# Keys of the last three batches: loaded in rows and turned over by DMA transpositions instead of TensorE

## The chip, the core and the metric

The kernel runs on one core of a Trainium2 chip. A core has five engines that run side by side and meet only at semaphores: TensorE (PE in the profile; its weight loads are shown apart as PEld), VectorE (DVE), ScalarE (ACT), GpSimd (POOL) and SyncE (SP), which here does nothing but issue transfers. Sixteen DMA engines carry the transfers. The metric is the time of one execution on the device, in microseconds (us); lower is better.

## The reference, cut to what matters

Attention over eight batches of eight heads, with 16 "beacon" keys and values put ahead of the 576 others, feeds a gated feed-forward network (called FFN below).

```python
B, H, S, Nb, D = (8, 8, 576, 16, 64)
k_all = concatenate([beacon_k, k], axis=2)          # 592 keys
v_all = concatenate([beacon_v, v], axis=2)
scores = scale * q @ k_all.T                        # causal; beacons are always seen
a = softmax(scores)
attn = a @ v_all
x = attn.transpose(0, 2, 1, 3).reshape(4608, 512)
out = (relu(x @ w_gate) * (x @ w_val)) @ w_out      # d_ff = 1536
```

Queries, keys, values and weights come from DRAM in float32; the kernel rounds them to bfloat16 for TensorE.

## The kernel before, in words

**One batch of attention.** `new_batch` makes the loads of a batch and what prepares them; `tile_step` and `group` do its scores, softmax and product with the values.

- Queries and keys are loaded by `load_pair`, one transfer for a pair of heads: 512 positions, four neighbouring positions of a head joined in one piece of 1 KB (L522). POOL rounds the tile to bfloat16 (`rounded`, L487), TensorE turns it over with four products with the identity (`turned`, L499), and ACT or DVE copies the result out of PSUM (`copy`, L439 for ACT, L441 for DVE) into `kT`, the transposed keys, or into `diag`, the queries of two heads set block-diagonally.
- The positions that `load_pair` leaves over come with `load_rest`: "first" holds 48 query rows and the 16 beacon keys (64 rows), "last" the last 64 keys and 16 queries (80 rows). Both go the same way: cast, four products of 64 or 80 columns, three copies.
- Values are loaded in rows by `load_v` (L596 to L599), in five chunks of up to 128 positions, each position with all eight heads: 128 pieces of 8 times 256 bytes. POOL rounds a chunk (L443), and it is used as it is.
- A step of scores (L657, L660, L665) multiplies queries by transposed keys. The query blocks are named A to D (of 128 positions), E (64) and F (the last 16 positions of all heads). AB sees up to 256 keys, C 384, D 512, E and F nearly all. DVE takes the row minimum (L677, L680), ACT the exponential and its sum (L691), DVE the inverse (L705), POOL scales (L712). A DMA transposition (L758) turns the probabilities `pb` of a pair of heads, 25 blocks of 128 by 128, into `pTb`; TensorE multiplies by the values (L768; L797 for F, from `pTf`), and ACT or DVE copies the result into `xT`.

**The FFN.** `hidden` (L835) multiplies `xT` by the gate and value weights, ACT applies the relu (L839), DVE multiplies (L843); `project` (L855) multiplies by the output weights, ACT or DVE copies to `osb`, and SP stores it (L868).

**What sets the order.** Nothing is run in the order in which it is written. Every piece is a task of `Plan` with the engines it may take, a booked cost, its dependencies, the buffers it holds, and a rank. `Plan.order` walks through booked time: of all tasks that could begin it takes the one that begins first, ties broken by rank. The result is one fixed order of instructions for each engine. An engine never goes past an instruction that waits. FFN tasks have ranks from 1000 up, so TensorE takes them when no attention is ready. `RANK` and `AHEAD` rank the loads and the preparing of a batch (the fourth entry serves batches 3 to 7), `WHOLE` and `F_RANK` its steps, `PACE` gives the earliest booked time of a step, `LAZY` is how long the planner lets a product with the values lie ready while other work can be had.

**Buffers.** Seven tiles `st` receive loads, three tiles `h16` hold rounded rows, there are two `kT`, two `diag`, two `v16`, three `pb`, three `pTb`, one `pf` and one `pTf`, and eight PSUM banks.

**Queues.** All loads, all transpositions and all but three stores are issued by SP, in one order. A transposition that waits for its source holds up everything behind it.

Of the kernel before, what the change touches and what calls it, by code (L numbers as in the profile page):

```python
# [10 lines left out]
BF16 = mybir.dt.bfloat16  # L11
# [6 lines left out]


BACKLOG = 3.0  # L20
EARLIER = {('g', 0): 3, ('v', 0): 4, ('g', 1): 2}
RANK = (-1.46, -25.77, -19.88, -17.37)
AHEAD = (-24.27, 8.0, -0.29, 8.0)
W_ISSUE = 0.8
W_MOVE = 3.1
W_FROM = 14.62
# [12 lines left out]
FILL_BANK = 36.0  # L39
SWITCH = 0.1  # L40
LAGS = {"PE": 0.22, "ACT": 0.16, "DVE": 0.14, "POOL": 0.1, "DMA": 0.1}
LAZY = 22.34
LAZY1 = 32.19
SLOT_LAZY = 0
ON_PE = 1
# [9 lines left out]
ORDER0 = "q0 q1 F k0 k1 k3 v1 q3 k2 q2 v2 v3 L v0 v4"  # L55
ORDER1 = "k0 F q0 k2 L k3 q2 v3 q3 k1 v0 v2 q1 v1 v4"
ORDER = "q0 k1 L k0 F q3 k3 q1 v1 k2 v0 v4 v3 q2 v2"
N_ST = 7
F_RANK = (6.53, 8.48, -1.67, 11.78)
CASTS = ('POOL', 'DVE')  # L60
N_OSB = 4
STEPS = {0: [(['AB'], (-4.55, -4.2, -4.25, -5.72)), (['C'], (-2.2, 4.89, 0.9, 1.36)), (['D', 'E'], (-0.26, 1.73, 10.1, -3.41))],
         1: [(['AB'], (4.7, -5.26, -1.44, -4.08)), (['C'], (8.45, 11.63, 1.33, -5.23)), (['D', 'E'], (3.48, 1.1, 9.61, 4.15))],
         2: [(['AB'], (6.63, 0.38, 0.63, -2.81)), (['C', 'D', 'E'], (6.95, 10.43, 5.74, -0.2))]}
WHOLE = (0.99, 5.23, 4.5, 5.2)
CUTS = {0: (240,), 1: (240,), 2: (240,), 3: ()}
LAST_PARTS = 2
FIRST_MOST = 4
PACE0 = 0.0
HOLD = {0: (0.0, 0.0, 0.0), 1: (0.0, 0.0, 35.39)}  # L70
PACE = 31.01


class Slots:
# [72 lines left out]
class Plan:  # L147
# [7 lines left out]
    def add(self, engines, cost, run, deps=(), holds=(), prio=0.0, lag=None, part=False, lazy=0.0, after=0.0, move=0.0):  # L155
        t = Task(engines if isinstance(engines, tuple) else (engines,), cost, run, deps, holds, prio, lag, part, lazy, move)
        t.ready = after
        for d in t.deps:
            d.users.append(t)
        self.tasks.append(t)  # L160
        return t
# [107 lines left out]
def kernel(  # L269
# [12 lines left out]
    nc = tc.nc  # L282
    B, H, S, D = q.shape
    Nb = beacon_k.shape[2]
# [3 lines left out]
    P = 128  # L288
    NP = H // 2
    SK = Nb + S  # L290
    NC = (SK + P - 1) // P
# [5 lines left out]
    neg_scale = -1.0 / (D ** 0.5)  # L297
# [17 lines left out]
    def many(n, shape, dtype, name):  # L315
        return [cp.tile(shape, dtype, name=f"{name}{i}") for i in range(n)]
# [4 lines left out]
    scales = cp.tile([P, 2], FP32, name="scales")  # L321
# [12 lines left out]
             for i in range(11)]  # L334
    p_t[0], pT_t[0], p_t[2], pT_t[2] = early[:3], early[3:5], early[5:8], early[8:]
    p_s, pT_s = [Slots(t) for t in p_t], [Slots(t) for t in pT_t]
    kT_s = Slots(many(2, [P, NP, SK], BF16, "kT"))
    v_s = Slots(many(2, [P, NC, DM], BF16, "v16"))
    diag_s = Slots(diag_t)
    stage_s = Slots(many(N_ST, [P, DM], FP32, "st"))  # L340
    outs = Slots(many(N_OSB, [P, DM], FP32, "osb"))
    osb_s = outs
    cast_s = Slots(many(3, [P, DM], BF16, "h16"))
# [8 lines left out]

    plan = Plan(BACKLOG)
    add = plan.add


    def c_dve(n):
        return 0.07 + 0.00104 * n
# [7 lines left out]
    def c_act(n):  # L366
        return 0.06 + 0.00083 * n
# [69 lines left out]
    def copy(e, dst, src):  # L437
        if e == "ACT":
            nc.scalar.copy(dst, src)  # L439
        elif e == "DVE":  # L440
            nc.vector.tensor_copy(dst, src)  # L441
        else:
            nc.gpsimd.tensor_scalar(dst, src, 1.0, 1.0, ALU.mult, ALU.mult)  # L443
# [17 lines left out]
    def heads(src, b, s0, sl):  # L461
        return src[b, :, s0:s0 + sl, :].rearrange("h s d -> s h d")
# [6 lines left out]
    def new_batch(b, prio, work):  # L469
        t = Batch()  # L470
        t.b = b
        t.kT = Hold(kT_s, 2 * (NP + 2) + NP * 4 + 1)
        t.v = Hold(v_s, NC + NP * (len(STEPS[b]) if b in STEPS else 2) + 1)
        t.diag = Hold(diag_s, 3 * NP + 6 + NP * 4 + 1)
        t.rows = {}
# [1 line left out]
        def rounded(into, st, rows, by, prio, ld, order):  # L477

            h16 = Hold(cast_s, 2)

            def shrink(x):
                to = order(h16.tile)[:rows]
                of = st.tile[:rows] if rows < P else st.tile.rearrange("p (h j d) -> p h j d", h=2, j=4)
                if x.engine == "ACT":
                    nc.scalar.activation(to, of, AF.Copy, scale=by)
                else:
                    (nc.gpsimd if x.engine == "POOL" else nc.vector).tensor_scalar(to, of, by, 1.0, ALU.mult, ALU.mult)  # L487

            return h16, add(eng, cost, shrink, (ld, on_scales), (st, h16, *into), prio[1])

        def turned(h16, rows, ca, prio, users):
            ps = Hold(first_ps if b == 0 else v_ps, 1 + users)
            deep = P if b else rows

            def turn(_):
                for a in range(4):

                    to = ps.tile[:, a * P:a * P + rows]
                    nc.tensor.matmul(to, h16.tile[:deep, a * P:(a + 1) * P], ident[:deep, :rows],  # L499
                                     start=True, stop=True)  # L500

            return ps, add("PE", c_pe(4 * rows), turn, (ca, on_ident), (h16, ps), prio[1])

        gate = (weight_in[GATE],) if b else ()
# [6 lines left out]
        eng = CASTS if b == 0 else ("POOL",)  # L511
        cost = {"POOL": 0.6, "DVE": 0.45, "ACT": 0.55}
        MAIN = 4 * P
        REST = S - MAIN
# [37 lines left out]
        def load_rest(kind, prio):  # L552

            st = Hold(stage_s, 2)
            own = 64 - Nb if kind == "first" else TAIL
            pieces = {"first": [(q, 0, own), (beacon_k, 0, Nb)], "last": [(k, MAIN, REST), (q, S - TAIL, own)]}[kind]
            rows = sum(x[2] for x in pieces)
            qs, ks = (0, own) if kind == "first" else (REST, 0)

            def fetch(_):  # L560
                s3 = st.tile.rearrange("p (h d) -> p h d", h=H)
                at = 0
                for src, s0, n in pieces:
                    gated(nc.sync.dma_start(s3[at:at + n], heads(src, b, s0, n)))
                    at += n

            ld = add("DMA", (1.05, 0.012 * rows if b else 1.55 if kind == "first" else 1.2, 8 * rows), fetch, gate, (st,), prio[0])
            i = 0 if kind == "first" else 1
            h16, ca = rounded((t.kT, t.diag), st, rows, scales[:rows, i:i + 1], prio, ld, lambda t_: t_)
            ps, tu = turned(h16, rows, ca, prio, 3)  # L570

            def evict_k(x):
                at = 0 if kind == "first" else Nb + MAIN
                n = rows - own
                copy(x.engine, t.kT.tile[:, :, at:at + n], ps.tile.rearrange("p (a n) -> p a n", a=NP)[:, :, ks:ks + n])

            def evict_q(x, hh):
                ps3 = ps.tile.rearrange("p (a n) -> p a n", a=NP)
                r = slice(64 * hh, 64 * hh + 64)
                at = 64 * hh + Nb if kind == "first" else NQ * P + TAIL * hh  # L580
                copy(x.engine, t.diag.tile[r, :, at:at + own], ps3[r, :, qs:qs + own])

            n = NP * (rows - own)
            t.rows["k", kind] = [add(("ACT", "DVE"), {"ACT": c_act(n), "DVE": c_dve(n)}, evict_k, (tu,), (ps, t.kT), prio[1])]
            n = NP * own
            t.rows["q", kind] = [add(("ACT", "DVE"), {"ACT": 0.06 + c_act(n), "DVE": 0.06 + c_dve(n)}, lambda x, hh=hh: evict_q(x, hh),
                                     (tu, on_zeros.get(b)), (ps, t.diag), prio[1]) for hh in range(2)]

        def load_v(c, prio):
            st = Hold(stage_s, 2)  # L590
# [11 lines left out]
            t.rows["v", c] = add(eng, cost, lambda x: copy(x.engine, t.v.tile[:rows, c, :], st.tile[:rows]),  # L602
                                 (ld,), (st, t.v), prio[1])

        for at, what in enumerate((ORDER0, ORDER1, ORDER)[min(b, 2)].split()):
            pr = (prio + 0.01 * at, work + 0.01 * at)
            if what in "FL":
                load_rest({"F": "first", "L": "last"}[what], pr)
            elif what[0] == "v":
                load_v(int(what[1]), pr)  # L610
            else:
                load_pair(what[0], int(what[1]), pr)
# [5 lines left out]
    def tile_step(t, p, name, ph, sc, prio, after, blocks):  # L618

        deps = [x for i in ([*range(NP)] if name == "F" else [p]) + (["first", "last"] if name in "EF" else ["first"])  # L620
                for kind in "kq" for x in t.rows[kind, i]]
        if name == "F":

            deps += [x_done[0, "AB", i] for i in range(NP)]
# [2 lines left out]
        if name in "EF":  # L627
            n = SK - TAIL if name == "E" else SK
# [7 lines left out]
        else:  # L636
            offs = [0, 0]
            for x in name:
                for hh in range(2):
                    n = P * FULL[x] + 64 * (hh + 1)  # L640
# [47 lines left out]
        for i, (n, hh, _, _, _, a) in enumerate(parts):  # L688
# [5 lines left out]
            need = [last[1]] if name in "EF" else [x for x, y in zip(lows, parts) if y[1] == hh]  # L694
# [185 lines left out]
    for b in range(B):  # L880
        batches.append(new_batch(b, RANK[min(b, 3)] + b * T0, AHEAD[min(b, 3)] + b * T0))
    for b in range(B):
        steps = STEPS.get(b, [(["AB", "C", "D", "E"], WHOLE)])
        for i, (names, ranks) in enumerate(steps):
# [9 lines left out]
    for b in range(B):  # L894
        hT = [Hold(hid_s, len(CUTS.get(b, ())) + 1 + REG // P) for _ in range(NF)]
        cuts = [0, *CUTS.get(b, ()), REG]
        prio = 1000 + 10.0 * b
# [8 lines left out]
    for i in range(2):  # L906
        b0, b1 = i * B // 2, (i + 1) * B // 2
        w = (b1 - b0) * (S - REG)
        prio = 1000 + 10.0 * b1 - 5.0
        hT = [Hold(hid_s, 1 + w // P + (LAST_PARTS - 1) * i) for _ in range(NF)]  # L910
        deps = [x for b in range(b0, b1) for x in done(b, REG, S)]
        hid = hidden(lambda ki, b0=b0, b1=b1: ends[:, ki, b0:b1, REG:], w, 0, deps, hT, prio)
        for t0 in range(0, w, P):
            b = b0 + t0 // (S - REG)
# [7 lines left out]
    order = plan.order()  # L922
    for i, (key, n) in enumerate(EARLIER.items()):
        at = order.index(weight_task[key])
# [38 lines left out]
```

## Time and profile before

| | before |
|---|---|
| median of 3 runs | 407.43 us (405.87 to 408.02) |
| the profiled execution, its time | 406.38 us |
| its span, first to last instruction | 404.7 us |
| mean granted TensorE clock | 0.999 |
| DVE, ACT, POOL busy | 78%, 72%, 58% |
| moved by DMA | 68.03 MB, mean 168 GB/s |

Between the time of an execution and its span lie 1.7 us before the first and after the last instruction.

How the views are read. The page gives the busy time of each engine and, in 40 slices, its share in tenths. The list of waits says who waited for whom and how long. The chain of waits follows the end of the kernel back, step by step, to what released it; in order of time its rows are start, length, and what ran ("PE f L835 x4" is four products of line 835 that write a PSUM bank f). Groups of instructions give count, busy time, and the mean of one in ns. "SPq" is SP's queue of transfers: the length of such a row is how long SP was taken by issuing it, and the time from issue to landing is listed apart.

### The profile page before, as it was taken

Reading aid. Unit: us, or ns where it says so; the run is one execution under the profiler, and the core shown is the slowest. Engines: PE = TensorE matmul, PEld = TensorE weight load, DVE = VectorE, ACT = ScalarE, POOL = GpSimd, SP = SyncE. Lnnn points to the kernel's source line nnn. Section 1 sums busy time; section 2 is a strip of 40 time slices with the busy share of each in tenths; the row PEclk is TensorE's granted clock in tenths of the full one; section 3 lists DMA queues with packets and bytes.
Section 4 is the critical chain, followed back from the end, with each engine's and each line's share of the span. In section 5 each row is a group of like instructions: output and inputs, shape, how many; then the busy total and the mean of one; then the engine's idle time right before and its main releaser. Section 6 shows DMA issues by size and latency. Waiting matters only on the chain.

```text
span 404.7 us, 10380 instructions
## 1 busy us (share of the span) xinstructions
PE 392.9 (97%) x3276; PEld 246.9 (61%) x3311; DVE 314.8 (78%) x1160; ACT 289.5 (72%) x958; POOL 233.9 (58%) x434
## 2 busy tenths in 40 slices
PE   7799999999999999999999999999999999999996
PEld 5567877587766877545558744554554545444484
DVE  7898999889989988899998998787988634233252
ACT  5799989789888968797988789998858433033030
POOL 5899885957777667687975966875737300000000
PEclk9999999999999999999999999999999999999999
DMA  7999999999889999999999999999296640110111
GB/s 230 181 232 217 222 173 189 198 240 213 178 183 228 214 181 236 183 228 200 247 204 198 231 212 188 252 200 198 71 164 126 152 90 0 53 52 0 53 52 54
DMA packets 172616, 68.03 MB, mean 168 GB/s; under 512 B 146832, under 2 KB 168080, under 8 KB 172560
## 3 DMA queue, kind: packets, MB, share of 16 engines
q1 hardware_dynamic: 167568, 62.38, 75.1%
q0 software_dynamic: 4752, 4.72, 7.2%
q8 instruction: 26, 0.43, 0.5%
q14 instruction: 30, 0.25, 0.2%
q10 hardware_dynamic: 240, 0.26, 0.2%
HBM read 38.27 MB, written 9.44 MB: 118 GB/s over the span
## 4 chain that ended last, share of the span: by engine, by line
PE 86%; POOL 5%; ACT 3%; issue 2%; DVE 2%; DMA 1%; SPq 0%; POOLq 0%; ACTq 0%; DVEq 0%
PE f L835 43%; PE f L855 22%; PE f L665 7%; PE f L768 5%; PE f L499 4%; ACT xT L691 2%; PE f L657 2%; POOL pb L712 1%; POOL xT L712 1%; PE f L919 1%; PE f L797 1%; DMA st<-in_beacon_k_dram 1%; POOL h L487 1%; PE f L660 1%; PE f L747 1%
## 5 line engine op out<-in xcount | busy, mean ns | idle before, releaser
L712 POOL TENSOR_SCALAR pb<-pb,small 128x576 bf16<-128x576 bf16 (+8 forms) x224 | 122.2, 562 | 54.9 <-DVE small L705 47.5
L691 ACT ACTIVATE pb<-f,small 128x64 bf16<-128x64 f32 (+6 forms) x256 | 131.3, 525 | 18.4 <-DVE small L680 14.3
L680 DVE CUSTOM_DVE_ANT_0 f<-f,mask 128x128 f32<-128x128 f32 (+7 forms) x256 | 111.7, 476 | 8.9 <-PE f L665 5.6
L839 ACT ACTIVATE g<-f 128x512 f32<-128x512 f32 (+3 forms) x156 | 72.1, 471 | 65.0 <-PE f L835 63.9
L835 PE MATMUL f<-xT,wv_r 128*128 128x512 bf16 (+3 forms) x616 | 111.8, 313 | 0.6
L835 PE MATMUL f<-xT,wg_r 128*128 128x512 bf16 (+3 forms) x619 | 109.5, 313 | 0.3
L843 DVE TENSOR_TENSOR hT<-g,f 128x512 bf16<-128x512 f32 (+3 forms) x156 | 80.2, 519 | 37.2 <-PE f L835 33.6
L855 PE MATMUL f<-wo_r,hT 128*128 128x512 bf16 (+1 forms) x423 | 102.0, 373 | 1.0
L835 PEld LDWEIGHTS <-wg_r 128*128 128x128 bf16 x624 | 60.0, 98 | 32.4 <-issue 0.3
L835 PEld LDWEIGHTS <-wv_r 128*128 128x128 bf16 x624 | 59.4, 98 | 32.8 <-issue 0.8
L855 PEld LDWEIGHTS <-hT 128*128 128x128 bf16 x444 | 41.6, 98 | 38.9
L691 ACT ACTIVATION_READ_ACCUMULATOR pb<-f,small 128x1 f32 x256 | 54.0, 211 | 0.0
L665 PE MATMUL f<-kT,diag 128*128 128x384 bf16 (+7 forms) x255 | 47.0, 286 | 1.6 <-DVE diag L441 0.5
L680 DVE DVE_READ_ACCUMULATOR2_ANT small<- 128x1 f32 x296 | 41.4, 140 | 0.0
L487 POOL TENSOR_SCALAR h<-st 128x512 bf16<-128x512 f32 x62 | 38.0, 620 | 3.3 <-DMA st<-in_q_dram 1.4
L441 DVE COPY osb<-f 128x512 f32<-128x512 f32 (+1 forms) x26 | 17.6, 677 | 23.1 <-PE f L855 22.7
L712 POOL TENSOR_SCALAR xT<-xT,small 128x64 bf16<-128x64 bf16 (+4 forms) x64 | 27.5, 448 | 9.1 <-ACT xT L691 4.0
L441 DVE CAST diag<-f 64x512 bf16<-64x512 f32 (+2 forms) x45 | 26.7, 592 | 4.0 <-PE f L499 1.4
L499 PE MATMUL f<-ident,h 128*128 128x128 bf16 (+3 forms) x320 | 27.9, 218 | 1.8 <-ACT pb L691 0.8
L439 ACT CAST diag<-f 64x512 bf16<-64x512 f32 (+2 forms) x51 | 22.7, 445 | 9.4 <-PE f L499 3.8
L665 PEld LDWEIGHTS <-diag 128*128 128x128 bf16 x256 | 20.4, 98 | 14.5 <-issue 1.4
L499 PEld LDWEIGHTS <-h 128*128 128x128 bf16 (+1 forms) x320 | 20.8, 99 | 13.9 <-POOL h L487 6.8
(67 smaller groups left out, 377.8 us busy)
## 6 DMA issues: line engine op xcount, KB each, us to landing
st<-in_q_dram SPq DMA_DIRECT2D x32, 256.0 KB, 4.1
st<-in_k_dram SPq DMA_DIRECT2D x32, 256.0 KB, 4.4
out_dram<-osb SPq DMA_DIRECT2D x32, 256.0 KB, 2.4
st<-in_v_dram SPq DMA_DIRECT2D x24, 256.0 KB, 4.6
st<-in_v_dram SPq DMA_DIRECT2D x8, 224.0 KB, 4.9
wg_r<-in_moe_w_gate_dram POOLq DMA_DIRECT2D x3, 512.0 KB, 6.8
wv_r<-in_moe_w_val_dram POOLq DMA_DIRECT2D x3, 512.0 KB, 10.0
wo_r<-in_moe_w_out_dram POOLq DMA_DIRECT2D x3, 512.0 KB, 10.6
```

The costliest lines, as they stand in the source:

```text
L439: nc.scalar.copy(dst, src)
L441: nc.vector.tensor_copy(dst, src)
L487: (nc.gpsimd if x.engine == "POOL" else nc.vector).tensor_scalar(to, of, by, 1.0, ALU.mult, ALU.mult)
L499: nc.tensor.matmul(to, h16.tile[:deep, a * P:(a + 1) * P], ident[:deep, :rows], start=True, stop=True)
L665: nc.tensor.matmul(view(i), t.diag.tile[:, p, j * P:j * P + P], kT[:, p, :n], start=True, stop=True)
L680: nc.vector.tensor_tensor_reduce(out=view(i), in0=view(i), in1=msk, scale=1.0, scalar=small["t"][:, 0:1] if name in "EF" else 3.0e38, op0= ...
L691: nc.scalar.activation(ph.tile.rearrange("p a n -> p (a n)")[:, a:a + n], view(i), AF.Exp, bias=small["t"][:, low:low + 1], scale=-1.0, ac ...
L712: (nc.gpsimd if x.engine == "POOL" else nc.vector).tensor_scalar(one, one, small["t"][:, 8 + i:9 + i], 1.0, ALU.mult, ALU.mult)
L835: nc.tensor.matmul(to, w_r[:, ki, nf * P:(nf + 1) * P], x, start=(ki == 0), stop=(ki == KM - 1))
L839: r = add("ACT", c_act(w), lambda _, psg=psg, g=g: nc.scalar.activation(g.tile[:, :w], psg.tile[:, :w], AF.Relu), (a,), (psg, g), -1000 + ...
L843: hid.append(add("DVE", c_dve(w), lambda _, psv=psv, g=g, nf=nf: nc.vector.tensor_mul(hT[nf].tile[:, c0:c0 + w], g.tile[:, :w], psv.tile[: ...
L855: nc.tensor.matmul(ps.tile[:, :w], hT[nf].tile[:, t0:t0 + P], wo_r[:, nf, n0:n0 + w], start=(nf == 0), stop=(nf == NF - 1))
```

## The change

For batches 5, 6 and 7 (`FROM = 5`) keys no longer go through `load_pair` and `load_rest`. They are loaded like values, in five chunks of up to 128 positions with all heads (`load_k`), rounded by POOL into an `h16` tile, and turned over by a DMA transposition of that tile, four blocks of 128 by 128, straight into `kT`. The tile `kT` is widened from 592 to 640 columns so that the last chunk fits. "First" and "last" carry queries alone in these batches (48 and 16 rows). A step of scores there depends on the key chunks it sees: AB on chunks 0 and 1, C on 0 to 2, D on 0 to 3, E and F on all five. A new order of loads (`ORDER_N`) serves these batches, and some ranks and planner numbers are changed; all ranks changed here serve batches from 3 on.

```diff
+ORDER_N = "q0 k1 q3 q1 k0 k3 v1 F k2 v3 L q2 v2 v0 v4"
+FROM = 5
+V_MOVE = 1.54
-RANK = (-1.46, -25.77, -19.88, -17.37)
-AHEAD = (-24.27, 8.0, -0.29, 8.0)
+RANK = (-1.46, -25.77, -19.88, 41.4)
+AHEAD = (-24.27, 8.0, -0.29, 57.18)
-LAZY = 22.34
+LAZY = 24.06
-F_RANK = (6.53, 8.48, -1.67, 11.78)
+F_RANK = (6.53, 8.48, -1.67, 23.02)
-WHOLE = (0.99, 5.23, 4.5, 5.2)
+WHOLE = (5.03, 5.84, 11.83, 8.03)
-PACE = 31.01
+PACE = 29.69
...
-    kT_s = Slots(many(2, [P, NP, SK], BF16, "kT"))
+    kT_s = Slots(many(2, [P, NP, NC * P], BF16, "kT"))
...
+            if b >= FROM:
+                pieces = [x for x in pieces if x[0] is q]
...
+        def load_k(c, prio):
+            st = Hold(stage_s, 2)
+            rows = min(P, SK - P * c)
+            def fetch(_):
+                s3 = st.tile.rearrange("p (h d) -> p h d", h=H)
+                if c == 0:
+                    nc.sync.dma_start(s3[:Nb], heads(beacon_k, b, 0, Nb))
+                    nc.sync.dma_start(s3[Nb:], heads(k, b, 0, P - Nb))
+                else:
+                    nc.sync.dma_start(s3[:rows], heads(k, b, P * c - Nb, rows))
+            ld = add("DMA", (1.1 if c == 0 else 0.55, V_MOVE * rows / P, 8 * rows), fetch, gate, (st,), prio[0])
+            h16 = Hold(cast_s, 2)
+            ca = add(eng, cost, lambda x: copy(x.engine, h16.tile[:rows], st.tile[:rows]), (ld,), (st, h16), prio[1])
+            t.rows["K", c] = [add("DMA", (1.22, 0.177 * NP), lambda _: nc.sync.dma_start_transpose(
+                t.kT.tile[:, :, P * c:P * c + P], h16.tile), (ca,), (h16, t.kT), prio[1] - 100.0)]
...
+            if b >= FROM and what[0] == "k":
+                load_k(int(what[1]), pr)
+                if what[1] == "3":
+                    load_k(4, pr)
...
+        if t.b >= FROM:
+            need = {"AB": 2, "C": 3, "D": 4}.get(name, NC)
+            deps += [x for c in range(need) for x in t.rows["K", c]]
```

The built program, counted without its times: TensorE has 48 instruction pairs (weight load and product) fewer, the 48 products of 128 columns that turned over 12 key tiles; 12 products shrink from 64 to 48 columns and 12 from 80 to 16. ACT and DVE lose 18 copies into `kT`. POOL has three casts more (15 key chunks for 12 key pairs). SP issues 15 transpositions more. The orders of all engines are the same as before up to a point about half way (TensorE: the scores of batch 4) and differ from there on.

More of the change, by code (lines that the diff above doesn't have):

```diff
@@ L471, in new_batch @@
         t.b = b
-        t.kT = Hold(kT_s, 2 * (NP + 2) + NP * 4 + 1)
+        t.kT = Hold(kT_s, (NC if b >= FROM else 2 * (NP + 2)) + NP * 4 + 1)
         t.v = Hold(v_s, NC + NP * (len(STEPS[b]) if b in STEPS else 2) + 1)
@@ L556, in load_rest @@
             pieces = {"first": [(q, 0, own), (beacon_k, 0, Nb)], "last": [(k, MAIN, REST), (q, S - TAIL, own)]}[kind]
+            if b >= FROM:
+                pieces = [x for x in pieces if x[0] is q]
             rows = sum(x[2] for x in pieces)
-            qs, ks = (0, own) if kind == "first" else (REST, 0)
+            qs, ks = (0, own) if kind == "first" else (0 if b >= FROM else REST, 0)
             def fetch(_):
@@ L568, in load_rest @@
             i = 0 if kind == "first" else 1
-            h16, ca = rounded((t.kT, t.diag), st, rows, scales[:rows, i:i + 1], prio, ld, lambda t_: t_)
-            ps, tu = turned(h16, rows, ca, prio, 3)
+            h16, ca = rounded((t.diag,) if b >= FROM else (t.kT, t.diag), st, rows, neg_scale if b >= FROM else scales[:rows, i:i + 1],
+                              prio, ld, lambda t_: t_)
+            ps, tu = turned(h16, rows, ca, prio, 2 if b >= FROM else 3)
             def evict_k(x):
@@ L583, in load_rest @@
             n = NP * (rows - own)
-            t.rows["k", kind] = [add(("ACT", "DVE"), {"ACT": c_act(n), "DVE": c_dve(n)}, evict_k, (tu,), (ps, t.kT), prio[1])]
+            if b >= FROM:
+                t.rows["k", kind] = []
+            else:
+                t.rows["k", kind] = [add(("ACT", "DVE"), {"ACT": c_act(n), "DVE": c_dve(n)}, evict_k, (tu,), (ps, t.kT), prio[1])]
             n = NP * own
@@ L587, in load_rest @@
                                      (tu, on_zeros.get(b)), (ps, t.diag), prio[1]) for hh in range(2)]
+        def load_k(c, prio):
[6 more added lines that the diff above has]
+                    nc.sync.dma_start(s3[Nb:], heads(k, b, 0, P - Nb))
+                else:
+                    nc.sync.dma_start(s3[:rows], heads(k, b, P * c - Nb, rows))
[4 more added lines that the diff above has]
+                t.kT.tile[:, :, P * c:P * c + P], h16.tile), (ca,), (h16, t.kT), prio[1] - 100.0)]
         def load_v(c, prio):
@@ L603, in load_v @@
                                  (ld,), (st, t.v), prio[1])
-        for at, what in enumerate((ORDER0, ORDER1, ORDER)[min(b, 2)].split()):
+        for at, what in enumerate((ORDER0, ORDER1, ORDER, ORDER_N)[3 if b >= FROM else min(b, 2)].split()):
             pr = (prio + 0.01 * at, work + 0.01 * at)
-            if what in "FL":
+            if b >= FROM and what[0] == "k":
+                load_k(int(what[1]), pr)
+                if what[1] == "3":
+                    load_k(4, pr)
+            elif what in "FL":
                 load_rest({"F": "first", "L": "last"}[what], pr)
@@ L620, in tile_step @@
         deps = [x for i in ([*range(NP)] if name == "F" else [p]) + (["first", "last"] if name in "EF" else ["first"])
-                for kind in "kq" for x in t.rows[kind, i]]
+                for kind in "kq" for x in t.rows.get((kind, i), [])]
+        if t.b >= FROM:
+            need = {"AB": 2, "C": 3, "D": 4}.get(name, NC)
+            deps += [x for c in range(need) for x in t.rows["K", c]]
         if name == "F":
```

## The prediction

> **What bounds the kernel now.** I read the page first, then the chain, then TensorE's waits, then the stretches that the change touches.
>
> ```profile
> span 404.7 us, 10380 instructions
> PE 392.9 (97%) x3276; PEld 246.9 (61%) x3311; DVE 314.8 (78%) x1160; ACT 289.5 (72%) x958; POOL 233.9 (58%) x434
> ...
> DMA  7999999999889999999999999999296640110111
> ...
> PE 86%; POOL 5%; ACT 3%; issue 2%; DVE 2%; DMA 1%; SPq 0%; POOLq 0%; ACTq 0%; DVEq 0%
> ```
>
> ```profile
> PE f L919 <- POOL mask L384: 1.9, 1, 1.9
> ...
> PE f L665 <- DVE diag L441: 0.5, 1, 0.5
> PE f L665 <- ACT diag L439: 0.5, 1, 0.5
> ```
>
> ```profile
> core 0: us, PE busy (x) PEld busy (x) DVE busy (x) ACT busy (x) POOL busy (x), PEclk, DMA share, GB/s
> ...
> 200.00:232.00 32.00, 31.84 (x326) 22.25 (x327) 29.19 (x115) 26.36 (x95) 24.16 (x44) 1.00 1.07 217
> 232.00:264.00 32.00, 31.84 (x244) 17.14 (x247) 28.17 (x103) 29.02 (x96) 23.01 (x45) 1.00 1.15 213
> 264.00:296.00 32.00, 31.79 (x237) 16.85 (x241) 26.14 (x101) 26.09 (x85) 21.99 (x41) 1.00 0.79 148
> 296.00:322.00 26.00, 25.78 (x183) 13.30 (x186) 19.90 (x77) 18.14 (x61) 12.09 (x22) 1.00 0.72 153
> ```
>
> TensorE carries 86% of the chain, and its longest waits after the start are two of 0.5 us, both on copies of queries. From 200 to 322 us, where batches 5 to 7 are worked on, it is idle for 0.75 of 122 us, at the full granted clock. Here a product taken away is time won, as long as TensorE finds its next input ready. The other resource near its limit is the transfers: their share is above 1 (packets overlap) until 264 us, 0.79 and 0.72 after. A late transfer does not show in the chain now, because FFN work stands ahead of each wait.
>
> **The change part by part.** *Products removed.* The chain in order of time has the price:
>
> ```profile
> 224.24 0.22 PE f L499 x4
> ...
> 229.97 0.48 PE f L499 x12
> ...
> 265.19 0.12 PE f L499 x4
> ```
>
> Four products of 128 columns take 0.22 us, four of 64 take 0.12 (265.19). The row of x12 holds groups of 128, 80 and 64 columns, so 80 columns cost 0.48 - 0.22 - 0.12 = 0.14. Twelve key tiles go: 12 x 0.22 = 2.64 us. Of "last", 80 columns become 16: between 0.14 - 0.12 = 0.02 (if 16 cost as much as 64) and 0.14 x 64/80 = 0.11 each; of "first", 64 become 48: 0 to 0.03 each. Three of both: 0.1 to 0.4. Products removed: 2.7 to 3.0; I take **-2.8 us**.
>
> *Copies removed, casts added.*
>
> ```profile
> L487 POOL TENSOR_SCALAR h<-st 128x512 bf16<-128x512 f32 x62 | 38.0, 620 | 3.3 <-DMA st<-in_q_dram 1.4 <-PE f L835 0.9 <-PE f L499 0.6
> ...
> L441 DVE CAST kT<-f 128x512 bf16<-128x512 f32 x18 | 12.2, 680 | 0.1
> ...
> L439 ACT CAST kT<-f 128x512 bf16<-128x512 f32 x14 | 8.3, 592 | 1.8 <-PE f L499 1.7
> ```
>
> The 12 large copies are 12 x 0.59 to 0.68 = 7 to 8 us of ACT and DVE. They shorten nothing that TensorE waits for beyond the two 0.5 us rows above: 0 to -1 us. I take 0, as both rows name queries, which stay. POOL gains 3 casts, 3 x 0.62 = 1.9 us, covered by its 41 idle us between 200 and 322 (122 less 81 busy): 0. Without that cover it would be 1.9.
>
> *Transfers.* Key bytes are the same, in smaller pieces:
>
> ```profile
> DMA packets 172616, 68.03 MB, mean 168 GB/s; under 512 B 146832, under 2 KB 168080, under 8 KB 172560
> ```
>
> ```profile
> st<-in_k_dram SPq DMA_DIRECT2D x32, 256.0 KB, 4.4
> ...
> st<-in_v_dram SPq DMA_DIRECT2D x24, 256.0 KB, 4.6
> ...
> st<-in_q_dram SPq DMA_DIRECT2D x8, 96.0 KB, 3.8
> pTb<-pb SPq DMA_TRANSPOSE x28, 6.2
> ...
> xT<-xT SPq DMA_TRANSPOSE x12, 3.5
> ...
> pTf<-pf SPq DMA_TRANSPOSE x7, 3.5
> ```
>
> ```profile
> L758 SPq DMA_TRANSPOSE pTb<-pb x28: 1494/3970/6172, 60.9 to 321.6; - x28
> L758 SPq DMA_TRANSPOSE xT<-xT x12: 1210/1261/2384, 54.1 to 116.0; - x12
> L758 SPq DMA_TRANSPOSE pTf<-pf x7: 1201/1271/2720, 76.3 to 304.6; - x7
> ...
> DMA to landing us min/median/max: 2.6/5.6/8.2
> ```
>
> A batch's 592 keys are 592 x 8 = 4,736 pieces of 256 B, where before 4 pair loads were 1,024 pieces of 1 KB and the 80 keys left over 640 of 256 B: 4,736 - 1,664 = 3,072 pieces more a batch, 9,216 in all, 5% of the 172,616 packets. Value chunks have exactly this shape and land after 4.6 us, key pairs after 4.4, so I price a key load 0.2 us later. A four-block key transposition is not in the trace. From below it cannot take SP less than 1.2 us, what the five-block `pTf` takes at least, or land before 2.6; from above 2.7 us on SP and 8.2 to landing, the worst rows. I take 1.27 and 3.5, the medians of five and six blocks. Fifteen of them are 19 us of SP over some 150. The last batch's attention ends some 10 us later in the new order, but with FFN work in between; what counts is whether each input is there when TensorE comes to it.
>
> *The new waits.* I laid the changed order of TensorE end to end at the chain's pace (four products of 512 columns in 0.86 us, others in proportion) and shifted it so that the old order, laid out alike, meets the old trace (18 to 19 us of start and gaps). This places instructions; the inputs' times are summed from rows:
>
> ```profile
> 222.61 0.47 SPq L564 DMA_DIRECT2D st<-in_q_dram  x1
> ...
> 234.57 1.19 SPq L868 DMA_DIRECT2D out_dram<-osb  x2
> ```
>
> ```profile
> 313.93 0.24 PE f L657 x2
> ...
> 341.15 1.50 PE f L768 x32
> ...
> 343.62 10.14 PE f L855 x47
> ```
>
> ```profile
> 319.06 0.75 POOL L712 TENSOR_SCALAR pb<-pb,small 128x576 bf16<-128x576 bf16 x1 [1.82 <-DVE small L705]
> ```
>
> From the last score of a pair (ends 314.17) to POOL's last scaling of it (ends 319.81) are 5.6 us: the link from TensorE to SP's transposition. A load issue is 0.47 us, a store 0.6, a 25-block transposition 3.97.
>
> - Batch 5, "first" queries: the last pair of batch 4 is scored to 195.6; +5.6 = 201.2. SP then issues a `pTb`, a `pTf`, two key transpositions, four stores and a value load ahead of "first": 3.97 + 3 x 1.27 + 2.4 + 0.47 = 10.7, so 211.9; +3.8 landing, +0.62 cast = 216.3. TensorE turns them at 217.9: **1.6 us to spare**.
> - Batch 7, third key chunk: a pair of batch 6 is scored to 281.1; +5.6, +3.97 for its transposition = 290.7; chunk 0 takes two issues, 4.6 and 0.62 to 296.9; then on SP its transposition, one `pTb`, two stores, two key transpositions: 1.27 + 3.97 + 1.2 + 2.54 = 9.0, so 305.9; +3.5 = 309.4. The first C scores stand at 311.6: **2.2 us**.
> - Batch 7, last values: the last pair is scored to 337.2; +5.6 + 6.2 = 349.0; its values stand at 349.8: **0.8 us**. Before, 27 us lie between these two (313.93 to 341.15), and 10 us of `project` for batch 6 stood behind the values (343.62). In the new order those products stand ahead of the last values, and behind them comes batch 7's own FFN: whatever is late here moves the end by as much.
>
> So margins shrink from tens of us to 0.8 to 2.2, each a sum of some eight links. I price waits at 0 if every sum holds, and up to 8.2 - 3.5 - 2.2 = 2.5 at the chunk and 2.0 (8.2 for 6.2) - 0.8 = 1.2 at the end. I take **+1.0** in all: near the lower end, because all three sums come out ahead.
>
> The sum is -2.8 + 1.0 = -1.8 on the profiled execution's 406.38, 404.6. The median of the runs, 407.43, lies 1.05 above that execution, so in its terms **405.6 us**.
>
> **The rivals.**
>
> - *No new wait.* The margins hold, and nothing else changes: -2.8, 404.6 against the median. For it: each sum is positive, and the shares of 0.79 and 0.72 leave room for transfers of batches 6 and 7. Against it: batch 5's keys are fetched at shares above 1.
> - *The gain is given back.* Waits of 2.8, by a link or two at their slow rows (a 25-block issue of 6.17 for 3.97 is in the list above): 407.4.
> - *SP's queue decides, slower.* Mechanism: a key transposition waits at the head of SP for POOL's cast, which waits for its load; loads and probability transpositions behind it start late, and the next scores with them. Before, only `pb` stood in this place. Price: if small transpositions hold SP for 2.72 (the worst row of `pTf`) and not 1.27, the first sum has three of them, 3 x 1.45 - 1.6 = 2.8 late, the second three, 4.35 - 2.2 = 2.2, and the end loses 1.2 as above: 6.2 - 2.8 = +3.4, 410.8. It decides from 1.27 + 1.6 / 3 = 1.8 an issue. For it: the 15 come among loads at a share above 1, and a fixed order cannot step aside. Against: the medians of the 19 small transpositions, in the same crowd, are 1.26 and 1.27.
> - *Small pieces are slow.* If 256 B pieces moved at half the rate, a batch's 1.2 MB of keys would take 2 x 1.2 MB / 213 GB/s = 11.4 us for 5.7. The 5.7 falls ahead of batch 7's third chunk: 5.7 - 2.2 - 2.8 = +0.7, 408.1; with batch 5's the same way (5.7 - 1.6) +4.8, 412.2. Against it: value loads land 0.2 us after key pairs. The Trainium skill, DMA: Bandwidth & Descriptors, Specifications, asks for at least 512 B a transfer for the full rate, and this change goes from 1 KB to 256 B; by that rule this rival is what happens, while the landing times here do not bear it out.
>
> **How the numbers follow.** 0.5% of 407.43, about what a measurement of this kernel can tell from no change, is 2.0 us. The forecast (waits of 0.2 to 2, 404.8 to 406.6) has 0.45, of which 0.12 with waits under 0.8 is faster and the rest no change. No new wait: 0.20, faster. Given back: 0.15, no change. SP's queue: 0.15, slower; small pieces: 0.05, slower. So faster 0.32, same 0.48, slower 0.20. The range reaches from 403.6 (no new wait, 1 us under the median as the profiled execution was) to 410.0, which leaves out the upper half of the slower cases.
>
> **What would show it.** L499's successor has 208 products of 128 columns for 256, and no copy into `kT` from the key groups of batches 5 to 7. Right: TensorE's waits stay under about 2 us after 200 us, on scores of batches 5 and 7 or the last values, and key transpositions land in 3 to 4 us. Wrong: waits of scores on a transposition into `kT` above 3 us together; SP held up at those transpositions by POOL's casts; key loads landing well after 4.6; an FFN product of batch 7 waiting for `xT`; or TensorE's time per turned tile far from 0.22.

## The result, and the profile after

| | before | after |
|---|---|---|
| median | 406.11 us (405.48 to 408.03, 11 runs) | 403.42 us (403.09 to 405.73, 11 runs) |
| the profiled execution, its span | 406.38, 404.7 us | 403.11, 401.1 us |

The ratio is 0.994, with a 95% interval from 0.9917 to 0.9962: about 0.6% faster, 2.7 us. Forecast and range were given for a kernel before at 407.43 us, whose median is 406.11 here, so they are best read as ratios: a range from 0.991 to 1.006 and a forecast of 0.9955. The measured ratio lies inside the range. In microseconds 403.42 lies 0.2 us under the range's lower end of 403.6 and 2.2 us under the forecast; 1.3 of these 2.2 are the other median of the kernel before, and 0.9 are the change, for which 1.8 us were forecast and 2.7 came.

First the two profiled executions have to be lined up, as their spans differ by 3.6 us and the medians by 2.7. Both orders are the same up to the scores of batch 4, so an instruction ahead of that point shows what the executions differ by without the change. Two rows of the chain of waits in order of time (start, length, what ran), of the kernel before: the last product of batch 3 with its values, and TensorE's last row.

```profile
171.14 0.60 PE f L797 x20
...
395.81 4.96 PE f L855 x34
```

The same two of the changed kernel, with rows for the small products that remain (16 columns, then 48) and for batch 7's last values:

```profile
170.40 0.60 PE f L831 x20
...
260.77 0.09 PE f L502 x4
...
303.12 0.10 PE f L502 x4
...
348.56 1.50 PE f L802 x32
...
392.50 4.96 PE f L889 x34
```

At the first the changed kernel is 171.14 - 170.40 = 0.74 us ahead, where the orders are still the same. (0.08 us of it stands at 81 us; the rest comes near 120 us, where the chain of the kernel before goes through a cast of POOL.) So it is a difference between two executions and not the change. At the last row it is 395.81 - 392.50 = 3.31 ahead. So 2.57 us were won where the orders differ, which is what the medians say. Four products of 16 columns ("last", 260.77) take 0.09 us and four of 48 ("first", 303.12) 0.10, against 0.14 and 0.12 for 80 and 64. Removed are thus 12 x 0.22 + 3 x (0.05 + 0.02) = 2.85 us, and at most 0.3 came back.

The page after, and TensorE's waits (who waited for whom: us in all, times, longest):

```profile
span 401.1 us, 10259 instructions
PE 389.0 (97%) x3228; PEld 243.0 (61%) x3263; DVE 309.6 (77%) x1149; ACT 286.5 (71%) x951; POOL 235.5 (59%) x437
...
DMA packets 189990, 69.97 MB, mean 174 GB/s; under 512 B 167280, under 2 KB 185456, under 8 KB 189936
```

```profile
PE f L502 <- POOL h L490: 1.4, 4, 0.5
PE f L502 <- ACT pb L725: 0.8, 1, 0.8
PE f L699 <- ACT diag L442: 0.5, 1, 0.5
PE f L699 <- DVE diag L444: 0.4, 1, 0.4
```

No score waits for a transposition into `kT`. When these waits occur matters more than their sums: all of them stand ahead of 62 us, long before the change. Asked from 175 us on, the list is empty for both kernels. By stretches (us, then busy time of PE, PEld, DVE, ACT, POOL with counts, granted clock, DMA share, GB/s):

```profile
200.00:232.00 32.00, 31.89 (x261) 20.68 (x262) 20.38 (x74) 15.04 (x55) 14.55 (x29) 1.00 1.02 202
232.00:264.00 32.00, 31.79 (x204) 15.86 (x207) 27.49 (x106) 27.37 (x91) 23.37 (x44) 1.00 0.89 173
264.00:296.00 32.00, 31.79 (x217) 16.18 (x221) 25.68 (x93) 27.41 (x84) 21.16 (x37) 1.00 1.08 210
296.00:322.00 26.00, 25.84 (x208) 13.97 (x211) 19.08 (x71) 16.13 (x59) 14.97 (x30) 1.00 0.73 153
322.00:364.00 42.00, 41.74 (x270) 20.44 (x273) 23.43 (x70) 20.71 (x60) 10.27 (x18) 1.00 0.52 108
```

From 200 to 322 us TensorE is idle for 0.69 us, against 0.75 before. Even this is not waiting: 35 products lack a record in either trace (3,228 beside 3,263 weight loads on this page), and a missing one leaves a short gap in this view. Meanwhile a good part of the attention has moved behind 322 (ACT is busy for 20.7 us from there to 364, 10.5 before). Of the packets, 17,374 more are seen than before; the keys' pieces make 9,216 of them.

How near the inputs come to their use is seen on SP's queue (start, time that the issue held SP, what was issued) ahead of batch 7's third key chunk, and in the products beside it:

```profile
296.90 4.00 SPq L792 DMA_TRANSPOSE pTb<-pb  x1
...
303.93 1.25 SPq L902 DMA_DIRECT2D out_dram<-osb  x2
...
305.28 3.85 SPq L613 DMA_TRANSPOSE kT<-h  x3
...
310.84 0.47 PE L699 MATMUL f<-kT,diag 128*128 128x320 bf16 x2
```

```profile
L613 SPq DMA_TRANSPOSE kT<-h x15: 1191/1230/2117, 186.8 to 307.9; - x15
...
DMA to landing us min/median/max: 2.4/2.9/6.0
```

The third transposition is issued at 307.9. With the median of 2.9 us it would land at 310.8; it took 2.5 itself, so it landed at 310.4. The first C scores start at 310.84, which leaves 0.4 us.

### The profile page after: what moved, and what is told of

It is laid out like the page before. It is cut to its first block, busy times and chain, and to the rows that moved or that the text cites. A ratio compares the mean times of both kernels' runs of the same rounds, so it can differ in the third digit from the quotient of the medians.

```text
span 401.1 us, 10259 instructions
## 1 busy us (share of the span) xinstructions
PE 389.0 (97%) x3228; PEld 243.0 (61%) x3263; DVE 309.6 (77%) x1149; ACT 286.5 (71%) x951; POOL 235.5 (59%) x437
## 2 busy tenths in 40 slices
DMA packets 189990, 69.97 MB, mean 174 GB/s; under 512 B 167280, under 2 KB 185456, under 8 KB 189936
## 4 chain that ended last, share of the span: by engine, by line
PE 81%; POOL 6%; DMA 4%; DVE 3%; ACT 3%; issue 2%; SPq 0%; POOLq 0%; DVEq 0%
PE f L869 41%; PE f L889 22%; PE f L699 6%; PE f L802 5%; DMA st<-in_v_dram 3%; PE f L502 3%; POOL pb L746 2%; POOL xT L746 2%; PE f L691 2%; ACT xT L725 2%; POOL h L490 1%; PE f L831 1%; DVE f L714 1%; DMA st<-in_beacon_k_dram 1%; PE f L694 1%
## 5 line engine op out<-in xcount | busy, mean ns | idle before, releaser
L746 POOL TENSOR_SCALAR pb<-pb,small 128x320 bf16<-128x320 bf16 (+8 forms) x224 | 122.2, 562 | 61.5 <-DVE small L739 56.7
L889 PE MATMUL f<-wo_r,hT 128*128 128x512 bf16 (+1 forms) x425 | 100.5, 373 | 0.9
L444 DVE COPY osb<-f 128x512 f32<-128x512 f32 (+1 forms) x29 | 19.7, 680 | 30.2 <-PE f L889 25.9
L490 POOL TENSOR_SCALAR h<-st 128x512 bf16<-128x512 f32 (+2 forms) x56 | 34.3, 619 | 6.1 <-DMA st<-in_k_dram 2.3
L446 POOL TENSOR_SCALAR v<-st 128x512 bf16<-128x512 f32 (+1 forms) x38 | 23.4, 620 | 19.0 <-DMA st<-in_v_dram 18.2
L711 DVE TENSOR_REDUCE small<-f 128x1 f32<-128x512 f32 x40 | 27.3, 683 | 2.2 <-PE f L694 1.4
```

The costliest lines, as they stand in the source:

```text
L711: nc.vector.tensor_reduce(out=to, in_=view(i), axis=AX.X, op=ALU.min)
L889: nc.tensor.matmul(ps.tile[:, :w], hT[nf].tile[:, t0:t0 + P], wo_r[:, nf, n0:n0 + w], start=(nf == 0), stop=(nf == NF - 1))
```

## The experiments

Theory A: the 2.7 us are TensorE's time for the products removed, and the rest of the change keeps waits away. Theory B: they come from the new ranks, or from the 18 copies that ACT and DVE no longer make.

The profiled executions begin at different speeds: among those whose order is still the same there, batch 3's last values (the row x20 above) start anywhere from 170.4 to 174.7 us. So beside the medians these are measured from that row's start to the end of TensorE's last product, called "the stretch" below. It takes 229.63 us in the kernel before (171.14 to 400.77) and 227.06 in the changed kernel (170.40 to 397.46).

**The products put back.**

```diff
...
+            if t.b >= FROM and name == "AB":
+                for _ in range(4):
+                    nc.tensor.matmul(view(3)[:, :P], t.diag.tile[:, p, :P], ident, start=True, stop=True)
             for i, (n, *_) in enumerate(parts):
```

> The changed kernel with 48 products of 128 columns added back on TensorE (four ahead of each pair's AB scores in batches 5 to 7, into a part of the bank that the scores then overwrite); they need nothing that the scores don't need, and every engine's order stays. Theory A (the gain is TensorE's time for the 48 products, 0.22 us for four): 12 x 0.22 = 2.6 us slower than the changed kernel, level with the kernel before (ratio 0.999 to 1.002). Theory B (the gain comes from the new ranks, or from the copies that ACT and DVE no longer make): the ratio stays near 0.994 to 0.996.

Measured: 1.0015 (0.9995 to 1.0036), 407.03 us. Level with the kernel before, and 0.75% above the changed kernel: 3.0 us for 48 products, where 0.22 us for four makes 2.6, and both intervals allow it. The trace says it more closely:

```profile
170.45 0.60 PE f L834 x20
...
394.89 5.22 PE f L892 x36
```

The stretch ends at 400.11 and takes 229.66 us: 2.60 more than in the changed kernel, and within 0.03 of the kernel before. No wait of TensorE is listed from 175 us on. ACT, DVE and POOL ran their changed orders unaltered, so ranks, copies and key path together give nothing beside the products. Theory A.

**The new ranks alone.** `FROM = 8`.

> The changed kernel with FROM = 8: no batch takes the new key path, all new ranks and planner numbers stay. Theory A: no gain, ratio 0.999 or above, as the 48 products are back and the ranks only place work. Theory B with the ranks as the cause: ratio near 0.994.

Measured: 1.0121 (1.0089 to 1.0153), 410.87 us. The ranks cost 4.9 us where keys still go over TensorE. The profiled execution (413.89 us) is the slowest of six, because it begins slowly: the stretch runs from 174.71 to 408.32, 233.61 us, 4.0 more than in the kernel before. TensorE's waits from 175 us on, and the windows with the idle time:

```profile
PE f L869 <- DVE diag L444: 0.7, 1, 0.7
PE f L502 <- ACT diag L442: 0.5, 1, 0.5
PE f L502 <- DVE diag L444: 0.3, 1, 0.3
PE f L502 <- DVE kT L444: 0.3, 1, 0.3
```

```profile
232.00:264.00 32.00, 30.59 (x212) 16.56 (x210) 29.00 (x115) 27.90 (x97) 24.27 (x46) 1.00 1.06 204
264.00:296.00 32.00, 30.88 (x235) 16.26 (x234) 27.23 (x98) 27.07 (x92) 22.42 (x43) 1.00 0.79 176
```

TensorE is idle for 2.5 us in these two windows, mostly waiting for copies of turned tiles by ACT and DVE. What the other 1.5 us are, the lists do not say. The list of the whole run would mislead: it has 5.0 us of waits for POOL's casts, and 4.8 of them stand ahead of 170 us, where the order is still that of the kernel before.

**The new path alone**, with the ranks and planner numbers of before.

```diff
-RANK = (-1.46, -25.77, -19.88, 41.4)
-AHEAD = (-24.27, 8.0, -0.29, 57.18)
+RANK = (-1.46, -25.77, -19.88, -17.37)
+AHEAD = (-24.27, 8.0, -0.29, 8.0)
...
```

> The changed kernel with the new key path for batches 5 to 7 and its order of loads, but RANK, AHEAD, LAZY, F_RANK, WHOLE and PACE of the kernel before. Theory A: the products are still gone (-2.6 to -2.8 us), and waits come on top where the old ranks leave no room for keys that come by DMA; between 0.994 (no waits) and 1.005 (some 5 us of waits on copies or transpositions of keys, queries or on late values). Theory B with the ranks as the cause: no gain, 1.000 or above, without new waits of TensorE.

Measured: 0.9999 (0.9982 to 1.0016), 405.95 us. The products are gone (3,263 weight loads for 3,311), and by the ratios the whole gain of 2.4 us is given back, give or take 1 us. In the profiled execution it is less: the stretch (172.94 to 401.67) takes 228.73 us, 0.9 less than in the kernel before and 1.7 more than in the changed one. TensorE's waits from 175 us on:

```profile
PE f L502 <- POOL h L490: 0.5, 2, 0.4
PE f L869 <- DVE xT L444: 0.3, 1, 0.3
```

These 0.8 us are half of the 1.7; where the rest is lost the list does not show. So the path needs the ranks and the ranks need the path: 1.7 us of the gain by the trace, all of it by the ratios, exist only because the order was made for it.

**The copies put back on ACT.**

```diff
                 low = 1 if name in "EF" else i
+                if t.b >= FROM and name == "D" and i == 1:
+                    nc.scalar.copy(ph.tile.rearrange("p a n -> p (a n)")[:, a:a + n], view(i))
```

> The changed kernel with 12 copies of 128x512 put back on ACT (one ahead of the last exponential of each pair's D step in batches 5 to 7, 0.59 us each, into a place that the exponential overwrites); order unchanged. Theory A: ACT is off TensorE's path, so 0 to 0.6 us slower than the changed kernel (0.994 to 0.996); the 0.6 where the last pair's chain has lost the little room it had. Theory B with the copies as the cause: most of the 2.7 us is given back, 0.998 to 1.001.

Measured: 0.9963 (0.9946 to 0.9979), 404.78 us: 0.9 us of the gain, with intervals that overlap the changed kernel's and allow anything from nothing to 2 us. The stretch (172.54 to 401.00) takes 228.46 us, 1.4 more than in the changed kernel, and one wait for ACT is new from 175 us on:

```profile
PE f L871 <- ACT pb L727: 0.5, 1, 0.5
```

So 7 us of ACT, put in these places, cost about 1 us: not the 2.7 of theory B, but not nothing either.

**Each key transposition issued twice.**

```diff
+            def turn_k(_):
+                nc.sync.dma_start_transpose(t.kT.tile[:, :, P * c:P * c + P], h16.tile)
+                nc.sync.dma_start_transpose(spare[c], h16.tile)
```

> The changed kernel with each of the 15 key transpositions issued a second time, into a tile that nothing reads; all other work and every other engine's order stay. SP is held 1.23 us more each time and the transfers move 128 KB more. Theory A' (the trace of the changed kernel shows next to no room at batch 5's 'first' queries and batch 7's third chunk: input and product fall together within 0.2 us): two more transpositions ahead of the one place and three ahead of the other, 2.4 + 3.6 us of waits, ratio about 0.994 + 0.015 = 1.009. Rival (the prediction's margins of 1.6 and 2.2 us are there): 0.9 + 1.5 = 2.4 us, ratio 1.000. Rival (SP's queue is nowhere on TensorE's path): 0.994.

Measured: 1.0252 (1.0214 to 1.0289), 416.16 us, 12.6 us above the changed kernel and twice what even theory A' expected. TensorE's waits from 175 us on, TensorE's windows around the first of them, and SP's issue of "first" for batch 5 (L570 here):

```profile
PE f L503 <- POOL h L491: 5.5, 3, 3.8
PE f L703 <- DMA kT<-h: 4.5, 2, 2.4
```

```profile
220.00:224.00 4.00, 0.23 (x5) 0.23 (x6) 0.42 (x1) 0.00 (x0) 1.23 (x2) 0.87 1.01 224
224.00:228.00 4.00, 4.00 (x26) 2.98 (x24) 1.66 (x9) 1.08 (x3) 2.87 (x5) 0.50 1.18 226
```

```profile
218.63 0.43 SPq L570 DMA_DIRECT2D st<-in_q_dram  x1
```

The waits are 10.0 us. The first of them, 3.8 us for the cast of "first", has a price of its own: it ends at 223.77, and from 224 to 228 us TensorE's granted clock was 0.50. Eight products of 256 columns took 1.91 us there (224.76), against 1.04 in the changed kernel (217.71):

```profile
224.76 1.91 PE L873 MATMUL f<-xT,wg_r 128*128 128x256 bf16 x8
```

```profile
217.71 1.04 PE L869 MATMUL f<-xT,wg_r 128*128 128x256 bf16 x8
```

From "first" to the values that follow it TensorE needs 6.26 us (223.77 to 230.03), where the changed kernel needs 3.38 (217.16 to 220.54): 2.9 us more. Waits and clock make 12.9 us together.

In the changed kernel the load of "first" was issued at 211.83. It is 6.8 us late here, but 2.7 of these stand ahead of any doubled transposition: SP issues the `pTb` ahead of batch 5's first key chunk at 185.00 here and at 182.27 there. The other 4.1 us are about three doubles, 3 x 1.26 = 3.8. I had counted the two that stand between the last probability transposition of batch 4 and the load; the double ahead of that transposition counts too, as SP had no pause between them, and the first of all fell into pauses of SP. So SP's time is on TensorE's path in batch 5 and again in batch 7.

**One transposition more, at one place.**

```diff
+                if b == 7 and c == 3:
+                    nc.sync.dma_start_transpose(spare, h16.tile)
```

> The changed kernel with one transposition more, into a tile that nothing reads, on SP between batch 7's key chunks 3 and 4, so 1.26 us ahead of chunk 2; all else as it is. Theory A' (chunk 2 lands just as its first C scores come up): TensorE waits 1.1 us more, at these scores, and the end is as much later: ratio 0.997. Rival (the prediction's 2.2 us to spare): no wait, 0.994.

Measured: 0.9961 (0.9939 to 0.9983), 404.74 us. The wait stands exactly where it was expected, in the list of waits and in the chain:

```profile
PE f L704 <- DMA kT<-h: 0.9, 1, 0.9
```

```profile
303.50 0.10 PE f L503 x4
...
309.62 2.47 DMA kT<-h
312.09 0.04 issue
312.14 0.47 PE f L704 x2
...
393.80 4.96 PE f L894 x34
```

1.26 us more on SP make 0.9 us of waiting at the C scores, so no more than 0.4 us were to spare there, against the prediction's 2.2. The wait reaches the end: like rows of the two chains stand 0.38 us apart ahead of it (303.50 and 303.12) and 1.30 at TensorE's last row (393.80 and 392.50). The ratios (0.9 us) and the medians (1.3 us) fit; the ratio's interval alone would also allow no change.

**More batches on the new path.** `FROM = 4` and `FROM = 3`.

> The changed kernel with FROM = 4: batch 4 takes the new path too. Theory A: 16 more products gone, 0.9 us less (ratio 0.992) if no wait comes instead. Against it: batch 4's keys travel where the DMA share is above 1; with waits of 1 us or more the ratio is 0.994 or above.

> The changed kernel with FROM = 3: batches 3 and 4 take the new path too. Theory A: 32 more products gone, 1.9 us less (ratio 0.9895) without waits. Against it: two more batches of transpositions and small pieces where the DMA share is above 1; waits of 2 us or more give 0.994 or above.

Measured: 1.0157 (1.0135 to 1.0179), 412.62 us, and 1.0589 (1.0566 to 1.0611), 430.19 us. In the first a single wait for a cast of queries lasts 6.5 us; in the second the values wait for the probabilities' transpositions:

```profile
PE f L502 <- POOL h L490: 7.0, 3, 6.5
```

```profile
PE f L802 <- DMA pTb<-pb: 18.7, 6, 6.1
...
160.00:200.00 40.00, 25.60 (x199) 13.83 (x201) 23.90 (x98) 20.76 (x76) 20.33 (x38) 0.79 1.09 200
```

The gain of 0.9 us a batch is nowhere to be seen under that. Whether ranks made for these orders would do better was not tried.

**A fourth `h16` tile.** `many(3, [P, DM], BF16, "h16")` becomes `many(4, ...)`.

> The changed kernel with four h16 tiles for three; the planner orders anew. If POOL's casts are held back by h16 tiles that wait for a transposition to land, the 1.4 us that TensorE waits for casts shrink: ratio 0.991 to 0.993. Rival: the casts are late because loads or SP are; no better than 0.994, or worse as the ranks were not made for this order.

Measured: 0.9967 (0.995 to 0.9984), 404.38 us, no gain. The run was meant to shorten the 1.4 us that TensorE waits for casts, and these stand ahead of 62 us; from 175 us on there is none to shorten, with three tiles or with four. Whether a fourth tile would help an order with ranks made for it is open.

**Stores off SP.**

```diff
-                if final and at:
+                if final and at or 1030 <= prio < 1070:
                     add("ACT", 0.6, store, (ev,), (osb,), prio + OUT)
```

> The changed kernel with the stores of the FFN of batches 3 to 6 issued by ACT (booked 0.6 us each there) instead of SP; the planner orders anew. Theory S (SP's issue time is what batches 5 to 7 are short of): some 18 issues of 0.5 us leave SP, the 1.4 us that TensorE waits for casts shrink; at most 1 us to win, ratio 0.991 to 0.994. Rival: ACT, now holding stores in its order, delays exponentials; ratio above 0.996.

> FROM = 4 with the stores of the FFN of batches 3 to 6 issued by ACT. Theory S: the 6.5 us wait of FROM = 4 comes from SP running late, so most of it goes and the ratio falls from 1.016 to 1.000 or below; without any wait it would be 0.992. Rival: the wait is made by POOL's order (casts of queries queued behind scalings that wait for DVE), which stores do not touch: the ratio stays above 1.008.

> Control: the kernel before with the stores of the FFN of batches 3 to 6 issued by ACT. Theory S: nothing on TensorE's path waits for SP there, so no gain: 0.999 to 1.003. Rival: the move of the stores is worth the same on either kernel (then e9 says nothing on the key path): as far below 1.000 as e9 is below 0.994.

Measured: 0.9938 (0.9916 to 0.9959), 403.83 us on the changed kernel; 1.019 (1.0145 to 1.0235), 414.34 us with `FROM = 4`; 1.0045 (1.002 to 1.0069), 407.64 us on the kernel before. By the ratios the move costs 1.8 us on the kernel before and nothing on the changed kernel, but the stretch grows by 1.0 us on either (230.63 and 228.04 us), so a difference between the two is not shown. `FROM = 4` is not saved by it. Its waits from 175 us on, the two longest:

```profile
PE f L502 <- POOL h L490: 2.9, 1, 2.9
PE f L802 <- ACT pb L725: 1.5, 1, 1.5
```

The wait of 6.5 us for a cast has shrunk to 2.9, and waits for ACT have come in its place. No version tried is clearly faster than the changed kernel.

## Why the prediction was right, and where it was off

- *What bounds the kernel.* Right. TensorE's time is the time: 2.57 us between like rows of the two chains against 2.85 removed, and the products put back, with everything else as it is, cost 2.60.
- *Products removed, -2.8.* Right, 12 x 0.22 and 0.2 for the smaller ones. Four products took 0.09 us at 16 columns and 0.10 at 48, so the smaller ones saved 0.05 and 0.02, within what was given.
- *Copies removed, 0.* Near enough: put back in the new order they cost 0.9 us by the ratios and 1.4 in the trace, where 0 to 1 was given. The reason given was weak. The two waits of 0.5 us that it rested on stand ahead of 20 us, and from 175 us on the kernel before has no listed wait, so they say nothing on batches 5 to 7.
- *New waits, +1.0.* This is the term that was mis-sized. No wait is listed from 175 us on, and at most 0.3 us came back (2.85 - 2.57). The case that came is the rival "no new wait", which had 0.20. The forecast "within 0.5%" was on the wrong side of its edge by 0.1%.
- *The three margins.* Their sums were right that it is tight and wrong about how much. For batch 5 the load of "first" was issued at 211.83 against 211.9 summed; it landed after 4.5 us where 3.8 was priced, its cast ended at 217.10, and TensorE came at 217.16 where 217.9 was laid out, so 1.6 us became 0.1. For batch 7's third chunk the sum missed a link: the two stores ahead of the key transpositions waited for their own products (SP left the `pTb` at 300.9 and issued the stores at 303.93, where the sum had them at 302.1). The transposition landed faster than priced (2.5 for 3.5 us), TensorE came 0.8 us earlier, and 2.2 became 0.4. For the last values the transposition was issued at 341.41 and landed after 5.6 us, at 347.0; the values stand at 348.56, so 0.8 became 1.5. That all three came out ahead is in part luck, as errors of up to 2 us went both ways and left 0.1 and 0.4. In part it is the work of the new ranks: with the ranks of before the same path loses 1.7 us (trace) to 2.4 us (ratios). The prediction treated the ranks as placing alone and gave them no price.
- *Rival "SP's queue decides".* Its mechanism is real, and its point lies close: key transpositions held SP for 1.23 us in the median, 1.8 was named as the point; at twice the time the kernel is 2.5% slower than before, not 0.8% (+3.4 us). SP was also held up at these transpositions by POOL's casts, for 5.4 us in all in the changed kernel, which was named as a sign of being wrong; no wait of TensorE came of it. The price lacked two things: TensorE waited at five places, not three, and ran at half its clock after the first wait.
- *Rival "small pieces are slow".* Not borne out. Key chunks land after 4.9 us in the median (L608), key pairs landed after 4.4: half a us later, where 0.2 was priced, not 5.7 for a batch. Not all of it is the pieces: query loads of 256 KB, whose pieces did not change, went from 4.1 to 4.4.

```profile
L608 SPq DMA_DIRECT2D st<-in_k_dram x12: 420/578/2400, 179.7 to 293.8; - x12
...
DMA to landing us min/median/max: 3.4/4.9/6.7
```

The rule of the Trainium skill that was weighed there (DMA: Bandwidth & Descriptors, Specifications: under 512 B no full rate) does not decide this case. These rows are landing times in a mixed queue, and no run here measures the rate of such pieces by itself.

## What to carry to other kernels

On a kernel whose busiest engine never waits, work taken off it is won nearly in full as long as the order puts every use behind its input, and a change of path without its order can give back most of the gain. Before a wait is made the cause of a loss, look at when it occurs: here the longest ones in whole-run lists stood ahead of everything that the change touches. When transfers replace instructions, add up the issuing queue: time that a queue spends on an issue comes back as waits of the engine once the queue has no pause ahead of it, and stores that wait at its head count like the issue itself. To learn how much room is left, add one dummy issue at one place and look for the wait.

## What the runs showed of the hardware

- A DMA transposition of 128 by 512 bfloat16 holds SP for 1.23 us and lands 2.9 us after its issue (medians of 15); issued directly behind another (the doubles) it holds SP for 1.26 and lands in 2.5. In the same run as the first, five-block `pTf` held SP for 1.23 and six-block `xT` for 1.26, so four blocks are hardly cheaper to issue than six.
- Bytes and packets rose by 1.94 MB and, beyond the keys' pieces, by 17,374 - 9,216 = 8,158 packets. That is 0.13 MB and 544 packets for each of the 15 transpositions, some 240 bytes a packet. The run with one more transposition has 544 packets more (190,534 for 189,990), the run with 15 more has 8,160 more (198,150).
- After longer waits TensorE's granted clock fell: to 0.50 from 224 to 228 us behind a wait of 3.8 us (doubled transpositions), and to 0.87 and 0.94 over 296 to 322 us with waits of 6.5 and 2.9 us in it (`FROM = 4`, without and with the stores moved). Over 160 to 200 us, with 14.4 us idle, it was 0.79 (`FROM = 3`). Behind waits of 2.4 and 2.1 us (doubled transpositions, in 264 to 296 and 322 to 364 us) it stayed at 1.00. The wait of 3.8 us was followed by 2.9 us lost to the slower clock.
